# Early loads of an FFT mixing kernel in another order, spread over sixteen DMA engines, in smaller reads, with the interleaving retimed

## The chip, the core and the metric

The kernel runs on one core of a Trainium2 chip. The time is the device time of one execution in microseconds (us), lower is better. One core has five engines that matter here: TensorE (PE in the profile; its weight loads are PEld), VectorE (DVE), ScalarE (ACT), GpSimd (POOL) and SyncE (SP). All share 16 DMA engines. A DMA is issued by SyncE, ScalarE or GpSimd, whose issues show as SPq, ACTq and POOL lines. In the DMA view, queue q0 carries what GpSimd issues, q1 what SyncE and q10 what ScalarE issues.

## The reference

For 8 images of 3136 tokens with 256 channels, a real Fourier transform over the tokens is multiplied by a filter and transformed back. Then comes a token mixer of rank 32, and a two-layer channel mixer with a residual:

```python
def _attn_ref(x, filt_r, filt_i):
    X = np.fft.rfft(x, axis=1)
    Y = X * (filt_r + 1j * filt_i)[None, :, :]
    return np.fft.irfft(Y, n=x.shape[1], axis=1).astype(np.float32)

def _moe_ref(x, U, V, w_ch1, w_ch2):                # x is the result of the above
    xt = x.transpose(0, 2, 1)
    h = xt @ U @ V                                  # rank 32 over the tokens
    u = x + h.transpose(0, 2, 1)
    ch = np.maximum(u @ w_ch1, 0.0) @ w_ch2         # 256 -> 1024 -> 256
    return (u + ch).astype(np.float32)
```

## The kernel before

3136 is 64 x 49, and both transforms are done as two stages of matmuls. The images go through in five units, counted from 0: image 1 alone is unit 0, image 2 alone is unit 1, then come three pairs. Each unit passes through these parts:

- **stage 1** (`f1`): load `x`, one matmul stage, store the result to a scratch tensor in DRAM (`ct1`; the trace writes `ct<-asb`, `ct<-al`).
- **mid stage** (`mid`): load it back as `a2` (in the trace `a<-ct`), multiply by the matrix `tf2`, multiply on VectorE by the filters `fab` (giving `uv`), multiply by the matrix `g3`, evacuate on ScalarE to `esb`, store to a second scratch tensor (`ct<-esb`). There are 32 such steps per unit.
- **low rank** (`low_rank`): load all of that unit back (`eh<-ct`), 24 matmuls into one small result, and two more copies, `hp` and `h1`.
- **groups**: the last inverse stage (`pu`, evacuated to `ut`), first channel matmul with ReLU (`phh`, `h`), second channel matmul (`pc`), store of the output. A unit has 7 groups if it is one image and 13 if it is two: g00 to g06 are image 1, g07 to g13 image 2, g14 to g26, g27 to g39 and g40 to g52 the pairs.

The groups are the steady work. Each full group has 8 steps, and a plan deals the next units' stage 1, mid stage and low rank onto these steps. For image 1 nothing can hide them: until its low rank is done there is no group to run.

These are the parts that the change and the argument touch. `hold(dst, src)` copies one element on VectorE, so that a load into `dst` can't be issued before `src` is there.

```python
def load_x(u, c, after=None):                       # x in 8 KB reads per row
    ...
        t = sb.tile([128, 8 * DM], F16, tag="x", bufs=4, name="x")
        if after is not None:
            hold(t[0:1, 0:1], after)
        nc.gpsimd.dma_start(t, dram(x.tensor, (u.b[0] * SEQ + 8 * c) * DM,
                                    [[NR * DM, 64], [st, 2], [1, 8 * DM]]))
def load_filters(a, z):                             # one of four parts of the filters, in pieces of 25 and 24 rows
    ...
def mirror_filters(a, z):                           # both halves once more, swapped: 1.6 MB inside SBUF
    nc.sync.dma_start(fab[0:NR, 1, a:z, :], fab[NR:98, 0, a:z, :])      # NR = 49
    nc.sync.dma_start(fab[NR:98, 1, a:z, :], fab[0:NR, 0, a:z, :])
load_filters(PARTS[0], PARTS[1])                    # part 0 at the very start, behind x
...
def second_loads(src):                              # at image 1's first a2
    for i in range(2, 4):
        load_part(i, src)                           # filter parts 2 and 3
    ...                                             # three small ones, then the rest of tf2 and g3
def third_loads(src):                               # at image 1's 11th multiply
    ...                                             # usb, vnat, w1sb, w2sb
# [f1: tf2 and g3 of the first 8 steps between the stage-1 stores; filter part 1 at stage 1's last evacuation]

# [low_rank, loads of image 1 in two parts]
if u.n == 0:
    a = 32
    for c in range(3):
        load(c, 0, a)
    load_l(0, a)
    yield
for c in range(3):
    load(c, a)
load_l(a)

# [main program, image 1]
for i in range(33):
    next(mids[0])
    if i == 24:
        next(ranks[0])                              # first part of the low-rank loads
...
next(ranks[0])                                      # second part
fourth_loads(units[0].held[64:65, 0, 0:1])          # x of image 2
...
hold(fab[0:1, 1, 0, 0:1], units[0].h1[64:65, 0:1])
hold(fab[64:65, 1, 0, 0:1], units[0].h1[64:65, 0:1])
mirror_filters(0, NK)                               # after image 1's h1

# [plan: generator, number of pieces, first step, last step; S = first step of each unit = 0, 49, 98, 196, 294]
deal(f1s[1], 7, 4, 11)
deal(mids[1], 33, 17, 33)
deal_f1(units[2], 12, (0, 2, 6, 7))
deal(mids[2], 33, 44, S[2] - 29)
deal_rank(units[1], 34, S[1] - 7)
deal_rank(units[2], S[2] - 28, S[2] - 7)
for u in units[3:]:
    deal_f1(u, S[u.n - 1] - (38 if u.n == 3 else 60), (1, 7))
    deal(mids[u.n], 33, S[u.n - 1] + (21 if u.n == 3 else 3), S[u.n] - 36)
    deal_rank(u, S[u.n] - 35, S[u.n] - 8)
```

## Time and profile before

| | |
|---|---|
| median of 3 runs | 629.87 us (628.38 to 631.92) |
| TensorE busy | 552.8 us, 88% of the span |
| TensorE's wait for image 1's low-rank loads | 10.3 us, ends at 65.4 |
| TensorE's wait behind image 2's x | 3.9 us, ends at 84.4 |
| TensorE's wait for the third low-rank loads | 10.5 us, ends at 248.6 |

The page of the kernel before cuts the span into 40 slices of 15.7 us. Each digit is a busy share in tenths. PEclk is the granted TensorE clock in tenths.

```profile
...
PE   3294576999699993989999999999999999999997
...
PEclk9558576999979997989999999999999999999999
DMA  9898979999835749868567787455433862331112
...
```

From the nineteenth slice on TensorE is full. The idle time lies before that, and there the DMA engines are full instead. The granted clock is 0.5 to 0.7 in seven of the slices up to the sixteenth, most of them slices in which TensorE idles or the next ones.

The view of waits gives, for one engine and a window, what the waiting line was released by: total us, number of times, longest. This is TensorE in the kernel before, from 60 to 180 us:

```profile
...
PE ph L476 <- DMA eh<-ct_0: 11.6, 3, 10.3
PE ph L476 <- DMA eh<-ct_1: 4.1, 3, 2.6
PE pf L304 <- DVE ut L539: 3.9, 1, 3.9
...
```

And the same view from 225 to 275 us:

```profile
...
PE ph L476 <- DMA eh<-ct_2: 10.5, 1, 10.5
...
```

Nearly all of it is the low rank waiting for its loads (`eh<-ct`). The third line is the start of stage 1 of a later unit behind a VectorE copy. What that copy waited for is seen in the chain and in VectorE's timeline below.

The chain of work that ended last, in order of time: start, length, what.

```profile
...
16.96 6.25 DMA ct_0<-al
23.25 4.47 DMA a_161<-ct_0
...
69.42 13.53 DMA x<-in_x_dram
...
```

The last store of stage 1 lands at 23.2 and the first load back starts. At 69.42 begins a load of x for image 2 that lands 13.5 us later.

In the view of the timeline a bracket gives the idle time before an instruction and what ended it.

```profile
...
83.05 0.14 DVE L174 COPY x<-x 1x1 f16<-1x1 f16 x1 [9.28 <-DMA x<-in_x_dram]
83.12 1.20 DVE L539 CAST ut<-pu 128x1024 f16<-128x1024 f32 x1
...
```

The one-element copy `x<-x` is the hold that lets the next unit's x load go only after image 2's third x tile. It waits 9.3 us for that tile, and the evacuation `ut` of the next group, ready by then, comes behind it in VectorE's program order.

### The profile page before, as it was taken

To read this page: it belongs to the slowest core of one execution; us is meant where nothing else is said; L and a number is where in the kernel's file an instruction comes from. 1 tells how busy PE (TensorE), PEld (TensorE's weight loads), DVE (VectorE), ACT (ScalarE), POOL (GpSimd) and SP (SyncE) were. 2 spreads that over 40 slices of the span, in tenths; PEclk is the share of its full clock that TensorE was granted. 3 is DMA by queue.
4 is the path that set the end of the run, shared out by engine and by line. 5 is a ranking of instruction groups with operands and counts; after the bars stand their busy time and mean duration, and the time that the engine had idled before them with its cause. 6 is when DMAs were issued, how large, how long until landed. Compare 5 with 4: busy or idle time off the path is not lost.

```text
span 629.3 us, 10769 instructions
## 1 busy us (share of the span) xinstructions
PE 552.8 (88%) x4350; PEld 388.0 (62%) x4350; DVE 330.0 (52%) x390; ACT 334.6 (53%) x623; POOL 41.7 (7%) x62
## 2 busy tenths in 40 slices
PE   3294576999699993989999999999999999999997
PEld 0183242767456661657766676777677767777776
DVE  5274222786278870263888743576866325333332
ACT  0043232667156662546667665665766655666663
POOL 3345110100000000000000000000000000000000
PEclk9558576999979997989999999999999999999999
DMA  9898979999835749868567787455433862331112
GB/s 176 230 205 193 214 183 236 246 250 244 244 119 161 216 81 286 208 166 227 171 187 173 208 245 249 156 148 187 120 131 119 239 202 83 99 100 67 66 67 102
DMA packets 68002, 110.18 MB, mean 175 GB/s; under 512 B 5549, under 2 KB 49438, under 8 KB 66604
## 3 DMA queue, kind: packets, MB, share of 16 engines
q1 hardware_dynamic: 36240, 81.17, 41.2%
q0 software_dynamic: 7312, 15.91, 15.8%
q10 hardware_dynamic: 24400, 12.41, 6.9%
q8 instruction: 34, 0.56, 0.4%
q14 instruction: 16, 0.13, 0.1%
HBM read 72.38 MB, written 51.38 MB: 197 GB/s over the span
## 4 chain that ended last, share of the span: by engine, by line
PE 73%; DMA 16%; issue 4%; DVE 3%; ACT 2%; ACTq 1%; POOL 0%; SPq 0%; POOLq 0%; DVEq 0%
PE phh L550 25%; PE pc L590 24%; PE pe L360 8%; PE pz L382 5%; PE pu L532 3%; PE pc L564 3%; DMA x<-in_x_dram 3%; PE pf L304 3%; DMA ct_3<-asb 2%; DMA g_78<-g 2%; DMA eh<-ct_1 2%; ACTq L320 1%; DMA eh<-ct_2 1%; DMA ct_0<-asb 1%; PE ph L476 1%
## 5 line engine op out<-in xcount | busy, mean ns | idle before, releaser
L550 PE MATMUL phh<-ut,w1sb 128*128 128x512 f16 (+2 forms) x848 | 251.7, 377 | 3.5 <-DVE ut L539 3.0
L397 DVE TENSOR_TENSOR uv<-pz,fab 98x1024 f16<-98x1024 f32 (+1 forms) x128 | 137.8, 1087 | 35.3 <-PE pz L382 34.8
L600 DVE COPY och<-pc 128x512 f32<-128x512 f32 x96 | 66.3, 690 | 165.8 <-PE pc L564 162.6
L550 PEld LDWEIGHTS <-w1sb 128*128 128x128 f16 x848 | 105.6, 146 | 36.7 <-issue 16.7
L366 ACT CAST esb<-pe 98x512 f16<-98x512 f32 (+1 forms) x160 | 79.5, 501 | 64.6 <-PE pe L360 57.0
L360 PE MATMUL pe<-uv,g_78 98*98 98x512 f16 (+1 forms) x320 | 85.7, 353 | 1.4 <-DMA g_78<-g 0.8
L539 DVE CAST ut<-pu 128x1024 f16<-128x1024 f32 (+1 forms) x51 | 59.9, 1174 | 21.6 <-PE pu L532 21.4
L564 PE MATMUL pc<-idn,ut 128*128 128x128 f16 x394 | 54.8, 220 | 0.0
L360 PEld LDWEIGHTS <-g_78 98*98 98x98 f16 x320 | 41.3, 132 | 19.4 <-issue 5.6
L564 PEld LDWEIGHTS <-ut 128*128 128x128 f16 x394 | 38.7, 98 | 6.7 <-issue 0.3
L382 PEld LDWEIGHTS <-tf_74 98*98 98x98 f16 x160 | 21.7, 136 | 20.2 <-DMA a_163<-ct_0 15.3
L304 PE MATMUL pf<-x,wf_64 128*128 128x512 f16 x84 | 27.9, 402 | 6.8 <-DVE ut L539 6.3
L476 PE MATMUL ph<-eh,ut_94 128*32 128x512 f16 (+1 forms) x120 | 10.7, 384 | 26.2 <-DMA eh<-ct_0 11.6
L167 POOL DMA_DIRECT2D x<-in_x_dram x24 | 14.1, 602 | 266.5 <-PE pf L304 225.1
L309 DVE CAST asb<-pf 128x1024 f16<-128x1024 f32 x21 | 25.6, 1219 | 11.5 <-PE pf L304 8.9
L307 ACT CAST asb<-pf 128x1024 f16<-128x1024 f32 x21 | 21.3, 1013 | 10.7 <-PE pf L304 6.7
L390 DVE TENSOR_TENSOR uv<-pz,fab 98x512 f16<-98x512 f32 x32 | 20.9, 687 | 5.1 <-PE pz L387 2.9
L476 PEld LDWEIGHTS <-ut_94 128*32 128x32 f16 x120 | 3.3, 97 | 31.6 <-issue 20.7
L366 ACT ACT_TABLE_LOAD x1 | 1.3, 1283 | 30.2 <-DVE uv L390 30.2
L382 PE MATMUL pz<-a_161,tf_74 98*98 98x256 f16 x8 | 3.2, 403 | 15.2 <-DMA a_163<-ct_0 14.9
L532 PEld LDWEIGHTS <-eb_97 96*128 96x128 f16 x256 | 10.3, 100 | 7.5 <-issue 4.7
L486 ACT CAST hp<-ph 128x512 f16<-128x512 f32 (+1 forms) x5 | 2.5, 501 | 23.1 <-PE ph L483 23.1
(1427 smaller groups left out, 1046.2 us busy)
## 6 DMA issues: line engine op xcount, KB each, us to landing
out_dram<-och SPq DMA_DIRECT2D x48, 512.0 KB
x<-in_x_dram POOLq DMA_DIRECT2D x24, 512.0 KB, 8.0
ct_2<-esb SPq DMA_DIRECT2D x16, 196.0 KB
ct_3<-esb SPq DMA_DIRECT2D x16, 196.0 KB
ct_4<-esb SPq DMA_DIRECT2D x16, 196.0 KB
ct_2<-asb ACTq DMA_DIRECT2D x6, 512.0 KB
ct_3<-asb ACTq DMA_DIRECT2D x6, 512.0 KB
eh<-ct_2 SPq DMA_DIRECT2D x6, 512.0 KB
```

Source lines behind the costliest of these rows:

```text
L304: nc.tensor.matmul(pf[:, i, :], wx, u.x[c][:, r:r + 2, :], start=True, stop=True)
L309: nc.vector.tensor_copy(dst, pf)
L360: nc.tensor.matmul(pe[0:98, 0:bd], g3[:, (2 * k + l) * 98:(2 * k + l + 1) * 98], uv[:, l * bd:(l + 1) * bd], start=(l == 0), stop=(l == 1))
L366: nc.scalar.copy(st["esb"][:, i, :], pe[0:98, 0:bd])
L382: nc.tensor.matmul(pz[0:98, 0:bd], wz, a2[c][:, i, :], start=True, stop=True)
L397: nc.vector.tensor_mul(uv.rearrange("p (f b d) -> p f b d", f=2, b=nb), zin, fin)
L532: nc.tensor.matmul(pu[:, dh, 64 * i:64 * i + 64], e2[0:96, d0:d0 + 128], sv[0:96, 64 * r:64 * r + 64], start=(i == 0), stop=True, skip_gro ...
L539: nc.vector.tensor_copy(gr.ut[:, :, 0:n].rearrange("p h (c q s) -> p h c q s", q=64, s=2), pu[:, :, 0:n].rearrange("p h (c s q) -> p h c q ...
L550: nc.tensor.matmul(ph[:, 0:n], w1v[:, dh, :, t], gr.ut[:, dh, 0:n], start=(dh == 0), stop=(dh == 1))
L564: nc.tensor.matmul(o[:, dh * 128:dh * 128 + 128], gr.ut[:, dh, t0:t0 + n], idn, start=False, stop=(dh == 1), skip_group_check=True)
L590: nc.tensor.matmul(o, gr.h[tt][:, i * 128:(i + 1) * 128], w2sb[:, tt * DM:(tt + 1) * DM], start=(tt == 0), stop=False, skip_group_check=True)
L600: nc.vector.tensor_copy(dst, gr.pc.rearrange("p (j d) -> p j d", j=2))
```

## The change

The intent is to take loads out of the crowded early stretches in which TensorE waits, to make each spread over more DMA engines, and to move pieces of the plan apart that seemed to collide:

- Start: filter part 0 and the first tf2 and g3 pieces come behind stage 1's last evacuation; filter part 1 at the first a2, parts 2 and 3 at the second and seventh multiply, the rest of tf2 and g3 at the first multiply. Filters load 24 rows and then one row. Half of the first unit's evacuations go to ScalarE.
- w1 and w2 are loaded late, behind the low-rank loads. Those come in three parts of 32, 16 and 16 rows.
- The mirror copies 48 rows and then one. x comes in 4 KB reads, two per tile. Two copies of h1 go to GpSimd.
- The plan is retimed, most of all for units 2 and 3.

```diff
 # load_x
+                hold(t[0:1, 4 * DM:4 * DM + 1], after)
+            for i in range(2):
+                nc.gpsimd.dma_start(t[:, 4 * i * DM:4 * (i + 1) * DM], ...   # [1, 4 * DM] per row
 # load_filters
-                fab[p0:p0 + 25, 0, a:a + n, :],
+                fab[p0:p0 + 24, 0, a:a + n, :],          # the 25th rows in load_filter_rows()
-    def mirror_filters(a, z):
-        nc.sync.dma_start(fab[0:NR, 1, a:z, :], fab[NR:98, 0, a:z, :])
-        nc.sync.dma_start(fab[NR:98, 1, a:z, :], fab[0:NR, 0, a:z, :])
+    def mirror_filters():
+        for a, z in ((0, 48), (48, NR)):
+            nc.sync.dma_start(fab[a:z, 1, :, :], fab[NR + a:NR + z, 0, :, :])
+            nc.sync.dma_start(fab[NR + a:NR + z, 1, :, :], fab[a:z, 0, :, :])
-    load_filters(PARTS[0], PARTS[1])
 # f1, unit 0
-                        nc.vector.tensor_copy(dst[:, i, :], pf)
+                        (nc.scalar.copy if i else nc.vector.tensor_copy)(dst[:, i, :], pf)
+        if u.n == 0:
+            first_loads(al[0:1, 0:1])                    # tf2 and g3 of the first 8 steps
+            load_part(0, asb[0:98, 4, 0:1])
 # mid, unit 0
-            second_loads(a2[0][0:1, 0, 0:1])
+            second_loads(a2[0][:, 0, 0:1])               # filter part 1 and three small ones
+            if u.n == 0 and k == 0:
+                second_matrices(uv[:, 0:1])              # the rest of tf2 and g3
+            if u.n == 0 and k in (1, 6):
+                load_part(2 if k == 1 else 3, uv[:, 0:1])
 # low_rank, unit 0
-            a = 32
-            for c in range(3):
-                load(c, 0, a)
-            load_l(0, a)
-            yield
+            for z in (32, 48):
+                for c in range(3):
+                    load(c, a, z)
+                load_l(a, z)
+                a = z
+                if z == 48:
+                    load_w1(eh[0][64:65, 0, 0:1])
+                yield
 # main program and plan                      (S = 0, 49, 98, 196, 294)
-        if i == 24:
+        if i in (22, 29):
             next(ranks[0])
-    deal(f1s[1], 7, 4, 11)
-    deal(mids[1], 33, 17, 33)
-    deal_f1(units[2], 12, (0, 2, 6, 7))
-    deal(mids[2], 33, 44, S[2] - 29)
+    deal(f1s[1], 7, 5, 12)
+    deal(mids[1], 33, 18, 34)
+    deal_f1(units[2], 17, (0, 2, 6, 7))
+    deal(mids[2], 33, 50, S[2] - 27)
-    deal_rank(units[2], S[2] - 28, S[2] - 7)
+    deal_rank(units[2], S[2] - 26, S[2] - 6)
     for u in units[3:]:
-        deal_f1(u, S[u.n - 1] - (38 if u.n == 3 else 60), (1, 7))
-        deal(mids[u.n], 33, S[u.n - 1] + (21 if u.n == 3 else 3), S[u.n] - 36)
-        deal_rank(u, S[u.n] - 35, S[u.n] - 8)
+        if u.n == 3:
+            deal_f1(u, S[2] - 38, (1, 7), (S[2] - 32, S[2] - 16))      # leaves out 16 steps
+        else:
+            deal_f1(u, S[u.n - 1] - 60, (1, 7))
+        deal(mids[u.n], 33, S[u.n - 1] + (40 if u.n == 3 else 3), S[u.n] - (30 if u.n == 3 else 36))
+        deal_rank(u, S[u.n] - (29 if u.n == 3 else 35), S[u.n] - 7)
 # [cut: ranks of unit 1 one step later; w2 and x held on other parts of eh; copies of h1 on GpSimd]
```

## The prediction

> **What bounds the kernel.** Median 629.87 us. The table of stages shows TensorE 99 to 100% busy from 300 us to 600 us (94% in 250 to 300): nothing to win there. The first 250 us hold nearly all of its idle time. The waits and the chain name it: 6.6 us for the first x; 15 us (12.6 to 27.9) for stage 1's stores and the a2 load; 10.3 us (55.1 to 65.4) for the low-rank load of the first image; 3.9 us at 80.5 behind the second image's x; about 6 us in 99 to 105, where ScalarE's queue is stuck issuing stores; about 6 us in 155 to 175 (second low-rank load, chain 9.9 us); 10.5 us before 248.6 (third low-rank load). After such gaps the granted clock is half: it is 0.61 in 27 to 50, 0.63 in 70 to 83 and 0.66 in 95 to 110.
>
> In these gaps the DMA engines are 80 to 100% busy, so order and spread of transfers matter, not compute.
>
> **What the change does.**
> 1. Start. In 9 to 24 us the filter loads hold 50% of the engines while the first stores, issued at 9.7, trickle until 14; the last store lands at 23.25. Part-0 and part-1 filters (0.8 MB in SBUF), tf2 and g3 parts (0.5 MB) now follow. Half the evacuations move from VectorE (0.68 us each, back to back) to ScalarE. Estimate: a2 loads 4 us earlier, stage 2 starts near 24.
> 2. First image's mid stage: filter parts stay just in time; g3 may again stall a microsecond or two (0.8 before). w1 and w2, which took most of the engines at 46 to 55 (software queue 52% in 46 to 62), leave that stretch. The last low-rank part shrinks from 32 to 16 rows. Estimate: low rank starts near 57 instead of 65.4, 8 us in all including step 1's 4.
> 3. The filter mirror: the trace's packets run on about 7 engines in 82 to 90. 49 rows give k = 7 and 48 give 16 (the Trainium skill, "DMA: Bandwidth & Descriptors", section on why a DMA increments its semaphore by 16), and this trace agrees. The x loads for image two (13.5 us in the chain) no longer share seven clogged engines. With the later stage 1 of unit 2 this recovers perhaps 6 of the 10 us lost in 80 to 110.
> 4. Retimed plan: a2 of unit 2 leaves the second low-rank stretch (4 us); unit 3's stage 1 skips the third one (8 us).
> 5. Costs: doubled x issues (0.58 us each, GpSimd, off the path); two 32x2048 copies on GpSimd instead of 0.68 us on VectorE, off the path; unit 2's mid stage is squeezed from 25 steps to 21 and unit 3's from 40 to 28, where 33 multiplies of 1.23 us bring VectorE to TensorE's level or above: 5 us lost. w2 and x now come late in a row: 3 us of new waits.
>
> Sum: 8 + 6 + 4 + 8 - 5 - 3 = 18, plus some 3 us from a clock that recovers earlier.
>
> **Prediction: 609 us, range 595 to 621 (8 in 10). Faster by over 2%: 0.77; within 2%: 0.20; slower: 0.03.**
>
> **What would show it.** First stage-2 matmul at about 24 us; first low-rank matmul about 57; mirror on the DMA view under 8 us; no wait over 3 us for the third low-rank load; more waits on VectorE's uv in the mid stages of units 2 and 3; TensorE busy time a little lower through the clock.
>
> **What would make it wrong.** New waits for filter parts or w1/w2; 2 KB x packets losing rate; the third low-rank load still late; gains given back because VectorE limits the squeezed mid stages.

## More of the kernel before

The order of instructions in the traces isn't exactly that of the plan; where it matters, it is read from the trace.

In the DMA view between 26 and 50 us, the columns after the count are KB and median us to landing:

```profile
...
fab<-in_filt_r_dram POOLq DMA_DIRECT2D x1, 100.0 KB, 7.7
...
fab<-in_filt_i_dram POOLq DMA_DIRECT2D x1, 84.0 KB, 13.1
...
```

Pieces of 84 to 100 KB take 8 to 13 us among the other loads of that stretch.

## The result, and the profile after

The changed kernel's median is 665.52 us (662.89 to 668.12, four runs), beside 629.36 for the kernel before. The ratio is 1.057 (95% interval 1.052 to 1.062): slower by 5.7%, where 3.3% faster had been predicted. The profiled executions were a little slow for their kernels (631.07 and 668.12 us), so the traces' spans differ by 37.0 us (629.3 to 666.3) where the medians differ by 36.2.

The slices of the page after are 16.7 us long:

```profile
...
PE   3257237699859999739999999899999999999997
...
PEclk9968577799969999868999999899999999999999
DMA  8896997869967545975788836853562563233112
...
```

TensorE's early idle time has grown, at slices 5 and 6, and the gap that was at slice 16 is now at 17 and 18, deeper in sum. TensorE's busy time rose by 10.8 us (552.8 to 563.6) for the same 4350 matmuls, and the other 26.2 of the 37.0 us are idle time. Where the longer busy time comes from wasn't followed up; the PEclk row shows lower clocks in slices 17 to 19, where the row of the kernel before has them in 16 and 18.

The waits of TensorE in the kernel after, from 60 to 180 us:

```profile
...
PE ph L499 <- DMA eh<-ct: 13.0, 1, 13.0
PE pf L328 <- DVE ut L562: 12.8, 1, 12.8
PE pz L398 <- DMA a<-ct: 4.1, 1, 4.1
...
```

And from 240 to 300 us, which holds the third low rank:

```profile
...
PE ph L499 <- DMA eh<-ct: 11.2, 5, 3.6
...
```

Not one of the waits that the change was meant for has gone. The first low-rank wait is 13.0 instead of 10.3 us, the wait behind image 2's x is 12.8 instead of 3.9, and the third low-rank wait is 11.2 in five pieces instead of 10.5 in one.

The chain of the kernel after, in order of time:

```profile
...
15.48 9.09 DMA ct<-asb
24.70 4.43 DMA a<-ct
...
59.19 5.51 DMA ct<-esb
67.32 2.66 DMA ct<-esb
70.59 5.63 DMA eh<-ct
79.70 21.19 DMA x<-in_x_dram
...
```

The next table gives milestones, read from the traces: starts of instructions, but ends for the two last multiplies; a group starts with its first ReLU. It is the map for all that follows. The first column is the kernel before, and the others are differences to it. The kernels e1 and so on are those of the experiments below; e14 and e13 each add to e5 alone. Every column is one execution. How far two executions of one program lie apart is seen in e15, whose instructions stand in the same order as those of the kernel before: -0.6 at g01, +2.4 at g07, +1.0 at g14 and +1.7 at g27. Differences of 2 to 3 us say little.

| us | before | after | e1: old plan | e5: + late mirror | e14: + early filters | e13: + two parts | e12: + both | e8: plan alone |
|---|---|---|---|---|---|---|---|---|
| image 1, first multiply | 28.5 | +1.5 | +2.7 | +1.8 | +1.0 | +2.1 | +0.6 | +0.2 |
| image 1, last multiply | 54.4 | +7.8 | +9.2 | +8.2 | +0.4 | +8.3 | +0.5 | +0.1 |
| first low-rank matmul | 65.4 | +10.2 | +10.8 | +11.4 | +6.0 | +5.7 | -0.6 | -0.2 |
| group g01 | 86.3 | +18.0 | +18.2 | +6.8 | +1.5 | +6.4 | -0.4 | -0.3 |
| group g07 | 176.7 | +23.8 | +23.0 | +9.4 | +8.9 | +8.2 | +2.4 | +4.0 |
| unit 2, last multiply | 229.1 | +30.9 | +21.9 | +8.7 | +8.0 | +8.1 | +1.6 | +11.1 |
| group g14 | 273.5 | +28.6 | +20.0 | +7.4 | +6.4 | +5.9 | +0.2 | +7.1 |
| group g27 | 403.5 | +37.1 | +18.7 | +7.0 | +6.1 | +6.1 | -0.7 | +14.4 |

Down the column of the kernel after there are three places where the loss grows: the mid stage of image 1 (about 8 us by its end, 10 with the low rank), the stretch to g01 (8 more), and from there on the units that the new plan moved (19 more). From g27 on nothing changes.

**The mid stage of image 1.** VectorE's timeline of the kernel after:

```profile
...
29.16 0.68 DVE L177 COPY fab<-a 1x1 f16<-1x1 f16 x4 [13.22 <-DMA a<-ct]
...
31.38 0.67 DVE L177 COPY fab<-uv 1x1 f16<-1x1 f16 x4
...
36.62 0.67 DVE L177 COPY fab<-uv 1x1 f16<-1x1 f16 x4
43.43 2.06 DVE L406 TENSOR_TENSOR uv<-pz,fab 98x512 f16<-98x512 f32 x3 [6.14 <-issue]
...
```

At 37.3 VectorE is done with the first eight multiplies and the holds for filter part 3. The ninth multiply needs part 1 of the filters, which could be issued only after the hold at 29.16. It comes 6.1 us late. The same is seen on GpSimd, whose bracket names the load:

```profile
...
31.32 0.66 POOL L199 DMA_DIRECT2D fab<-in_filt_i_dram  x1
...
43.95 0.70 POOL L199 DMA_DIRECT2D fab<-in_filt_i_dram  x1 [5.15 <-DMA fab<-in_filt_i_dram]
...
```

Part 1's four pieces are issued from 29.59 to 31.98, and part 2 and most of part 3 right behind. The issue at 43.95 waited 5.2 us for a filter piece to land. By the DMA view of this stretch the pieces took 8 to 12 us (medians), much as in the kernel before. Part 1's own four took 3.0, 3.2, 6.2 and 12.0 us: the last one, issued at 31.32, landed at 43.35, and the multiply began at 43.43. In the kernel before part 1 had been issued from 15 us on, and the wait did not exist.

**The low rank of image 1.** SyncE's timeline, its issues alone, in the kernel before:

```profile
...
53.85 2.24 SPq L368 DMA_DIRECT2D ct_0<-esb  x3
61.62 1.80 SPq L448 DMA_DIRECT2D eh<-ct_0  x3
...
```

And in the kernel after:

```profile
...
59.19 0.98 SPq L384 DMA_DIRECT2D ct<-esb  x2
...
64.75 1.84 SPq L468 DMA_DIRECT2D eh<-ct  x3
...
67.32 0.34 SPq L384 DMA_DIRECT2D ct<-esb  x1
...
69.99 1.81 SPq L468 DMA_DIRECT2D eh<-ct  x3
...
```

Before, SyncE issues the last stores of the mid stage in a row, and the second half of the low-rank loads waits for them alone. After, the second part (64.75) waits for a store of 59.19 to land, and the last store (67.32), which has nothing to do with it, is issued only behind it, by SyncE's program order. The third part waits for that store in turn (69.99). The chain shows just these pieces: store 59.19, store 67.32, load 70.59. From the last multiply to the first low-rank matmul the kernel before takes 11.0 us and the kernel after 13.5.

**Image 2's x.** VectorE's timeline after:

```profile
...
100.98 0.20 DVE L177 COPY x<-x 1x1 f16<-1x1 f16 x2 [19.04 <-DMA x<-in_x_dram]
101.11 1.20 DVE L562 CAST ut<-pu 128x1024 f16<-128x1024 f32 x1
...
```

The hold waits 19.0 us for x, and behind it `ut` is late, which is TensorE's 12.8 us. The x tile was issued at 79.7 instead of 69.4, since the low rank was late, and then took 21.2 instead of 13.5 us. The DMA view of the stretch 88 to 94 gives each queue's packets, MB and share of the 16 engines:

```profile
...
q1 hardware_dynamic: 67, 0.80, 90.5%
q0 software_dynamic: 65, 0.12, 16.4%
...
```

q0 is x, q1 almost only the mirror. The mirror holds 90% of the engines, and x gets 0.12 MB in 6 us, in about as many packets (65 and 67).

**The plan.** In unit 2 the plan deals the mid stage onto fewer steps (21 instead of 25); in the trace it starts at 205.9 instead of 171.1 and ends at 259.9 instead of 229.1. From its end to g14 both kernels need much the same time (44.4 us before, 42.2 after), so the later end is passed on. In unit 3 the same happens again. The view of stretches gives start and end, the length, then the busy us (and instructions) of PE, PEld, DVE, ACT and POOL, the granted clock, the DMA share and GB/s. For 55 us of unit 2's mid stage, before:

```profile
...
175.00:230.00 55.00, 53.90 (x344) 33.30 (x344) 46.62 (x44) 34.27 (x66) 1.00 (x2) 0.94 0.51 150
...
```

And after:

```profile
...
205.00:260.00 55.00, 54.28 (x359) 33.75 (x359) 46.53 (x44) 34.47 (x66) 1.19 (x2) 1.00 0.49 144
...
```

VectorE is no busier after the change than before it (46.5 and 46.6 of 55 us), and TensorE is full in both.

### The profile page after: what moved, and what is told of

Same layout as the page of the kernel before. It is cut to its first block, busy times and chain, and to the rows that moved or that the text cites. A ratio compares the mean times of both kernels' runs of the same rounds, so it can differ in the third digit from the quotient of the medians.

```text
span 666.3 us, 10847 instructions
## 1 busy us (share of the span) xinstructions
PE 563.6 (85%) x4350; PEld 390.0 (59%) x4350; DVE 327.6 (49%) x401; ACT 338.2 (51%) x630; POOL 61.2 (9%) x90
## 4 chain that ended last, share of the span: by engine, by line
PE 67%; DMA 21%; DVE 5%; ACT 3%; issue 2%; POOL 1%; SPq 1%; ACTq 0%; DVEq 0%; POOLq 0%
PE phh L573 23%; PE pc L613 20%; PE pe L376 8%; DMA eh<-ct 7%; PE pz L398 5%; DMA x<-in_x_dram 4%; DMA ct<-al 3%; PE pf L328 3%; PE pc L587 3%; PE pu L555 3%; DMA ct<-esb 2%; DMA a<-ct 2%; DVE eb L441 2%; DMA ct<-asb 1%; DVE ut L562 1%
## 5 line engine op out<-in xcount | busy, mean ns | idle before, releaser
L576 ACT ACTIVATE h<-phh 128x512 f16<-128x512 f32 (+2 forms) x424 | 237.1, 566 | 169.7 <-PE phh L573 164.4
L613 PE MATMUL pc<-w2sb,h 128*128 128x256 f16 x1536 | 242.1, 276 | 1.0 <-ACT h L576 1.0
L613 PEld LDWEIGHTS <-h 128*128 128x128 f16 x1536 | 146.6, 99 | 74.1 <-issue 7.4
L376 PE MATMUL pe<-uv,g 98*98 98x512 f16 (+1 forms) x320 | 84.8, 351 | 0.6 <-ACT esb L382 0.4
L398 PE MATMUL pz<-a,tf 98*98 98x512 f16 (+1 forms) x160 | 56.4, 355 | 27.6 <-DMA a<-ct 18.4
L376 PEld LDWEIGHTS <-g 98*98 98x98 f16 x320 | 41.1, 133 | 18.7 <-issue 4.7
L555 PEld LDWEIGHTS <-eb 96*128 96x128 f16 x768 | 32.5, 100 | 17.7 <-DVE eb L441 6.4
L328 PE MATMUL pf<-x,wf 128*128 128x512 f16 x84 | 27.8, 403 | 14.5 <-DVE ut L562 14.1
L555 PE MATMUL pu<-sv,eb 96*128 96x64 f16 x768 | 35.7, 197 | 5.0 <-DVE eb L441 3.7
L499 PE MATMUL ph<-eh,ut 128*32 128x512 f16 (+1 forms) x120 | 11.2, 408 | 32.9 <-DMA eh<-ct 32.7
L398 PEld LDWEIGHTS <-tf 98*98 98x98 f16 x160 | 21.5, 135 | 22.7 <-issue 16.2
L331 ACT CAST asb<-pf 128x1024 f16<-128x1024 f32 x21 | 21.3, 1013 | 15.5 <-PE pf L328 15.3
```

What stands on the lines that cost most here:

```text
L328: nc.tensor.matmul(pf[:, i, :], wx, u.x[c][:, r:r + 2, :], start=True, stop=True)
L376: nc.tensor.matmul(pe[0:98, 0:bd], g3[:, (2 * k + l) * 98:(2 * k + l + 1) * 98], uv[:, l * bd:(l + 1) * bd], start=(l == 0), stop=(l == 1))
L398: nc.tensor.matmul(pz[0:98, 0:bd], wz, a2[c][:, i, :], start=True, stop=True)
L555: nc.tensor.matmul(pu[:, dh, 64 * i:64 * i + 64], e2[0:96, d0:d0 + 128], sv[0:96, 64 * r:64 * r + 64], start=(i == 0), stop=True, skip_gro ...
L576: nc.scalar.activation(h[:, 0:n], ph[:, 0:n], RELU)
L613: nc.tensor.matmul(o, gr.h[tt][:, i * 128:(i + 1) * 128], w2sb[:, tt * DM:(tt + 1) * DM], start=(tt == 0), stop=False, skip_group_check=True)
```

## The experiments

I took the reading above as theory A: the loss has three sources, the loads of image 1, the mirror beside x, and the plan, and the plan costs time on its own. The rival B for each source was that it does not cost by itself but only passes on a lateness made elsewhere. For the plan in particular B says that the new plan still helps, and that only a late start hides it. The letters in the texts stand for the theory under test and its rival in that run.

In the short diffs, a minus line is of the kernel after (or before, where said), and the plus line what the experiment has in its place. The times are medians; each ratio is against the kernel before in the same rounds, with its 95% interval.

### e1: the old plan under the new loads

```diff
-    deal(f1s[1], 7, 5, 12)        # and all other lines of the new plan
+    deal(f1s[1], 7, 4, 11)        # the plan of the kernel before, unchanged
```

> The changed kernel with only the retimed plan (the steps at which later units' stages are dealt out) put back to that of before; everything of the early loads stays changed. Theory A (the retimed plan itself costs: the mid stage of unit 2 starts 10.9 us later than the groups around it, the low-rank stage of units 2 and 3 then ends late): some 13 us back, about 652 us. Theory B (the plan fits the new loads and saves, the loss is all in the first 110 us): time rises by up to 10 us, to 668 to 676 us.

Measured: 646.86 us, 1.027 (1.019 to 1.035). The new plan costs about 18.7 us of the 36. In the table the +18.2 of g01 is +23.0 at g07 and +18.7 at g27: under the old plan a late start is in the end neither recovered nor made worse. The filter wait is there too, and here the bracket on VectorE names it (line numbers are of this kernel):

```profile
...
44.91 2.06 DVE L442 TENSOR_TENSOR uv<-pz,fab 98x512 f16<-98x512 f32 x3 [6.43 <-DMA fab<-in_filt_i_dram]
...
```

### e2: the mirror with 49 rows again

```diff
-        for a, z in ((0, 48), (48, NR)):
+        for a, z in ((0, NR),):
```

> The changed kernel with the filter mirror back in two transfers of 49 rows. Theory A (spread over 16 engines with 16 KB packets, the mirror starves the second image's x loads, which landed at 101 us, 21 us after the issue): x lands near 92 us, about 657 us in all. Theory B (x is late because its 2 KB packets lose against any larger ones, or because w2 stands in front of it): unchanged within 2 us, 664 to 668 us.

Measured: 660.80 us, 1.048 (1.039 to 1.056), and g01 at +17.4 instead of +18.0. I had suspected that the mirror crowds x out because it now runs on all engines. That falls: on seven engines x is as late, with the third tile at 100.4. A gain of some 5 us appears only later in the program; I can't explain it, and end to end it is not clear of the noise (1.048 against 1.057, 1.0% on either side).

### e3: the low-rank loads in two parts

```diff
-            for z in (32, 48):
+            for z in (32,):            # w1 then held on the first part
```

> The changed kernel with the first image's low-rank loads in two parts as before (w1 held on the first part). Theory A (the loads of the second of three parts stand on SyncE's in-order queue ahead of the last store of the mid stage, which is ready at 62.9 us and issued at 67.3): first low-rank matmul 3 to 5 us earlier than 75.6 us, about 661 us in all. Theory B (the last part is shorter with three parts, so the split saves): 666 to 670 us.

Measured: 661.00 us, 1.049 (1.043 to 1.054). The run doesn't tell what it should. To keep w1 late I held it on the first part, and that hold sat on VectorE in the middle of the mid stage, so image 1's last multiply came at +12.6 instead of +7.8. What two parts gained was lost there. e13 does this properly.

### e4: the filters in the old order

```diff
+    load_filters(PARTS[0], PARTS[1])   # at the start, and parts 1 to 3 where they were before
-            load_part(0, asb[0:98, 4, 0:1])
```

> The changed kernel with the filters, tf2 and g3 loaded when and in the row counts they were before (25 and 24 rows), all else changed. Theory A (putting filters and matrices late moved no store forward and made the mid stage wait: 4.2 us on VectorE's multiply, 2.4 us on tf2): first multiply near 28.5 us, no wait over 1 us in the first mid stage, about 659 us in all. Theory B (the stores gain as intended and the late start comes from elsewhere): 666 us or more.

Measured: 655.11 us, 1.039 (1.033 to 1.046). Image 1's last multiply is at +1.2 instead of +7.8, and g01 at +11.6 instead of +18.0. The late loads are shown to be the cause of the loss in the mid stage. This edit, and those of e13 and e14, puts back tf2, g3, the row counts and the number of holds together with the time of the filters; "late filters" below stands for all of it. The bracket in e1 names a filter piece. The first multiply came at 29.7, beside 30.1 with late filters and 28.5 before: there was no gain to lose at the start.

### e5: old plan, and the mirror after x

The mirror is held on the third x tile of image 2, and issued later in the program order.

```diff
-    hold(fab[0:1, 1, 0, 0:1], units[0].h1[64:65, 0:1])
-    hold(fab[64:65, 1, 0, 0:1], units[0].h1[64:65, 0:1])
-    mirror_filters()
 # in the step loop, after unit 2's first load_x
+    hold(fab[0:1, 1, 0, 0:1], units[1].x[2][0:1, 0, 0:1])
+    hold(fab[64:65, 1, 0, 0:1], units[1].x[2][64:65, 0, 0:1])
+    mirror_filters()
```

> The run with the old plan (646.9 us) with one thing more: the filter mirror waits for the second image's third x tile to land, as its result is first read some 30 us later. Theory A (x and mirror share the engines packet by packet, and the mirror's 16 KB packets leave little to x's 2 KB ones: x drops to 20 GB/s beside it): x lands near 90 us instead of 101, about 638 us in all. Theory B (x is late by w2 and its own order alone): no change, 645 to 649 us.

Measured: 639.41 us, 1.018 (1.013 to 1.022). The x tile lands at 90.2, g01 is at +6.8 instead of +18.2, and end to end 0.9% of the time is won against e1 (1.018 against 1.027). In the DMA view of 82 to 92 us the queues have changed places:

```profile
...
q0 software_dynamic: 980, 1.69, 91.8%
q1 hardware_dynamic: 95, 0.51, 16.9%
...
```

Now x has 92% of the engines and moves 1.69 MB in 10 us. The mirror beside x is the cause of the loss between 80 and 101 us.

### e6: x in 8 KB reads again, with the old plan

```diff
-            for i in range(2):         # two reads of 4 KB
+            for i in range(1):         # one of 8 KB
```

> The run with the old plan (646.9 us) with x back in single reads of 8 KB (4 KB packets in SBUF). Theory A (packet size sets x's share beside the mirror): x lands 3 to 6 us earlier than 101 us, about 642 us in all; the start is unchanged or up to 1 us earlier. Theory B (packet size is harmless): 645 to 649 us.

Measured: 649.73 us, 1.032 (1.027 to 1.036), against e1's 1.027: no gain. Yet the packets tell why x yields to the mirror. This is a sum over the trace's packet records in the two halves of 88 to 96 us, with the mirror running in all three kernels:

```
                     x: packet size, rate              queue with the mirror: packet size, rate
e1 (4 KB reads)      1.8 KB, 18 to 25 GB/s             12 to 13 KB, 140 to 153 GB/s
e6 (8 KB reads)      3.7 to 3.9 KB, 37 to 58 GB/s      11 to 12 KB, 129 to 176 GB/s
e2 (4 KB, 49 rows)   1.3 to 1.7 KB, 18 to 41 GB/s      8 to 13 KB, 136 to 145 GB/s
```

The Trainium skill, "DMA: Bandwidth & Descriptors", section "Queues, rings and completion order", says that each DMA engine goes round the queues for which it has work, one packet each. By that, x would get 1.8 of every 1.8 + 12.5 KB, an estimate of 13%, with the small reads, and 3.7 of 3.7 + 12.5 KB, 23%, with the large ones. The runs show 11 to 14% and 22 to 25%. So the 4 KB reads did halve x's share beside the mirror. But x landed only 2.1 us earlier with the large reads (99.0 against 101.1), and it had also been issued 2.1 us earlier (77.7 against 79.8). From issue to the landing that the hold waits for, both took 21.4 us, though in e6 that is the whole tile and in e1 its first half. The 2.1 us were lost again by the start of unit 3 (its first a2 load: +19.1 against e1's +18.6). The larger share is shown, a gain of time is not.

### e7: all loads of image 1 in the old order, old plan

```diff
 # e1, and the filters as in e4, and the low rank in two parts as in e3
```

> The run with the old plan (646.9 us) with filters, matrices and low-rank loads back in their old order and parts; late w1 and w2, x in 4 KB reads, the 48-row mirror and the moved copies stay. If the first mid stage's waits and the three parts cost the 8.8 us seen at the first ReLU: about 637 us, first ReLU near 74 us or earlier, since w1 and w2 no longer fill the engines. If late w1/w2, x reads or the mirror cost it: 643 us or more.

Measured: 640.75 us, 1.018 (1.012 to 1.025). The hold of w1 on the first part costs here as in e3: the trace shows VectorE stopped from 49.6 to 54.5, and TensorE with it from 50.2 to 55.3. g00 came at +3.7 and g01 at +12.7. The direction is clear, the size is not. e12 repeats it without this fault.

### e8: the new plan alone on the kernel before

```diff
 # kernel before
-    deal(f1s[1], 7, 4, 11)        # and all other lines of the old plan
+    deal(f1s[1], 7, 5, 12)        # the plan of the kernel after
```

> The kernel before with the retimed plan alone. Theory A (the plan's loss of 18.6 us is its own, independent of the loads): about 648 us. Theory B (the plan only fails on top of late early loads): 630 us or less.

Measured: 645.92 us, 1.027 (1.024 to 1.030). This settles the matter of the plan: with none of the other changes, and image 1 as early as before, the plan alone costs 2.7%. The wait that it was to avoid is back as five waits:

```profile
...
PE ph L537 <- DMA eh<-ct: 11.0, 5, 3.4
...
```

From the table: unit 2's last multiply is 11.1 us late, g14 7.1 us, g27 14.4 us. TensorE's idle time, summed from the instruction records between milestones, shows the exchange: from g07 to g13 it falls from 11.4 us in the kernel before to 0.8, but from g13 to g14 it rises from 2.3 to 15.3, and from g20 to g27 from 0.0 to 3.7.

### e9: the late mirror alone on the kernel before

```diff
 # kernel before, with the change of e5
```

> The kernel before (629 us) with one thing changed: the filter mirror, still 49 rows, waits for the second image's third x tile. Theory A (mirror and x collide in the kernel before too, there for the 3.9 us that TensorE waits behind x at 80.5): x lands near 80 us instead of 83, 3 to 4 us in all, about 626 us. Theory B (the collision only hurts where x comes late): 628 to 631 us; if the mirror then comes too late for the next mid stage, more.

Measured: 633.83 us, 1.003 (0.9995 to 1.007): nothing gained. g01 came 4.3 us earlier, as it should, since x landed at 79.1 instead of 83.0. But the mirror then ran while ScalarE was issuing the stores of stage 1. Two lines of ScalarE's timeline:

```profile
...
88.36 15.62 ACTq L366 DMA_DIRECT2D ct<-asb  x2
104.03 1.01 ACT L353 CAST asb<-pf 128x1024 f16<-128x1024 f32 x1 [15.19 <-issue]
...
```

ScalarE spent 15.6 us on issuing two stores, and its next evacuation waited behind them. TensorE's waits show it:

```profile
...
PE pf L376 <- ACT asb L353: 13.2, 1, 13.2
...
```

That moving the large transfer out of one collision moved it into another is my reading. The mirror's packets ran from 81.0 to 99.9, through most of this time. But in the kernel before, too, ScalarE's issues of two such pairs, from 93.7 on and with the mirror over since 91.1, took 4.1 and 5.2 us beside x of the next unit. How much of the 15.6 us is the mirror's is not shown.

### e10 and e11: the new plan of unit 2 alone, and of unit 3 alone, on the kernel before

```diff
 # e10, kernel before
-    deal_f1(units[2], 12, (0, 2, 6, 7))
-    deal(mids[2], 33, 44, S[2] - 29)
-    deal_rank(units[2], S[2] - 28, S[2] - 7)
+    deal_f1(units[2], 17, (0, 2, 6, 7))
+    deal(mids[2], 33, 50, S[2] - 27)
+    deal_rank(units[2], S[2] - 26, S[2] - 6)
 # e11, kernel before: the lines of the new plan for u.n == 3
```

> The kernel before with only unit 2's part of the retimed plan (stage 1 five steps later, mid stage from step 50 to 71 instead of 44 to 69, low-rank stage 2 steps later). Theory A (the low-rank chain follows the end of the mid stage, so a mid stage that ends later ends the unit later, whatever waits it avoids before): 3 to 5 us slower, about 633 us. Theory B (the loss in the plan-only run is from the one-step shifts of unit 1): within 1.5 us of before.

> The kernel before with only unit 3's part of the retimed plan (stage 1 skips 16 steps, which pushes the mid stage from steps 119 to 159 to steps 138 to 166, low-rank stage 6 steps later). Theory A: the 10.5 us wait before unit 2's low-rank matmuls shrinks, but unit 3's low-rank stage ends late and gives back more, about 7 us slower in sum, 636 us. Theory B (removing the wait is worth its length): 620 us.

Measured: e10 637.83 us, 1.009 (1.004 to 1.013); e11 637.96 us, or 637.53 without its slow execution, 1.006 (1.001 to 1.012). Both halves cost. In e11 my idea worked at first: with unit 3's stage 1 out of the way, g13 starts 8.6 us earlier and g20 9.7 us earlier than in the kernel before. The gain is given back in unit 3, whose mid stage now ends 11.6 us later, and g27 is 7.3 us late. Together they are 1.5%, beside 2.7% for the whole plan, a difference of 1.2% with 0.8% on either side. In the traces nothing is missing: at g27 they are +6.7 and +7.3, together 14.0, beside e8's +14.4. Neither edit has the one-step moves of unit 1 and of the end of units 3's and 4's low rank, but in e10's trace unit 1's mid stage already stands in e8's order. So the two halves account for all, or nearly all, of the plan's loss; what the other moves add is not resolved.

### e12: old loads, old plan, late mirror, with the rest of the change left in

```diff
 # kernel after with the old plan, the filters in the old order, the low rank in two parts, the late mirror,
 # and w1 held on the last low-rank part:
+        if u.n == 0:
+            load_w1(eh[0][64:65, 0, 0:1])      # after the second part is issued
```

> What is left of the change once the plan, the filter order and the three low-rank parts are back as before and the mirror waits for x: late w1 and w2 (w1 held on the last low-rank part, not in the middle of the mid stage as in the two earlier runs with two parts, where that hold stalled VectorE for 5 us), x in 4 KB reads, 48 rows, the evacuations and copies moved to other engines. If plan, filter order, three parts and mirror collision are all the causes: first ReLU at 74 us as before and 625 to 630 us. If late w1 and w2 or the rest cost by themselves: 633 us or more.

Measured: 631.30 us, 0.999 (0.994 to 1.003). What is left in it (x in 4 KB reads, evacuations on ScalarE, w1 and w2 late, the mirror of 48 rows, copies on GpSimd) neither costs nor gains as a whole. The first low-rank matmul comes at 64.7, beside 65.4 in the kernel before, so taking w1 and w2 out of the stretch before it gained nothing that the traces resolve. The sum can hide opposite parts, and the traces show some. In e9 and e12 the mirror comes after x, and x is asked for from 68.4 and 68.2 us. In e9 the third tile was there at 79.1 and g01 came 4.3 us early; in e12, where x stands behind w2 and comes in 4 KB reads, the tile was there at 82.2 and g01 came 0.4 us early. And TensorE waited 1.8 us for w1. I ran none of these parts alone.

### e13 and e14: one of the two returned at a time

```diff
 # e13: e12 with the filters late, as in the kernel after
 # e14: e12 with the low rank in three parts, as in the kernel after
```

> The late-mirror run (old plan, 639.4 us) with the first image's low-rank loads in two parts and w1 held on the last part, so that no hold stands in the mid stage; the new filter order stays. Theory A (three parts cost some 3.4 us, as SyncE's queue keeps the last store behind a load that waits): about 636 us, gap from the mid stage's end to the first low-rank matmul 11 us instead of 14. Theory B (the filter order alone makes the 8 us between 639.4 and 631.3): 639 us.

> The late-mirror run (old plan, 639.4 us) with the old filter and matrix loads, three low-rank parts kept. Theory A (filters cost 5 us, parts 3.4): about 634.5 us. Theory B (filters alone): 631 us, as the run with both undone (631.3).

Measured: e13 637.28 us, 1.011 (1.008 to 1.014); e14 634.36 us, 1.006 (1.002 to 1.009). Beside e12, the late filters add 7.8 us at the end of image 1's mid stage (+8.3 against +0.5 in the table). The three parts add 6.6 us at the first low-rank matmul without delaying the mid stage at all. With both, in e5, that matmul is at +11.4. Of the 6.6 us of e14 only 1.9 are left at g01, and at g27 they are 6.8; how they grow again in between I didn't resolve. The profiled execution of e14 was the slowest of its six, 2.5 us above their median. As with the filters, the edit of the three parts brings small things with it (where `u_hat` and the holds of w1 and w2 stand).

The ratios of e1, e5, e13, e14 and e12 give the bill. The interval of a step, worked out from those of its two ratios, is 0.9% on either side for the first two steps and 0.6% for the others. The runs also come from several chips, each beside its own kernel before.

| step | ratio before | ratio after | part of the time |
|---|---|---|---|
| new plan undone (after to e1) | 1.057 | 1.027 | 3.0%, 19 us |
| mirror moved behind x (e1 to e5) | 1.027 | 1.018 | 0.9%, 6 us |
| filters in the old order (e5 to e14) | 1.018 | 1.006 | 1.2%, 8 us |
| low rank in two parts (e14 to e12) | 1.006 | 0.999 | 0.7%, 4 us |

The us are the percentages of 629 us. In this order the steps lead back to the time of the kernel before. End to end the mirror's step is only just clear of the noise; what shows it is x's landing and g01 in the traces of e1 and e5. Taken the other way round, from e5 to e13 to e12, the parts are worth 0.7% and the filters 1.2%: within the noise the two add up.

### e15 and e16: the opposite of the new plan

If an earlier end of unit 2's mid stage is what the third low-rank wait needs, it must start earlier rather than later.

```diff
 # kernel before; e15, and in brackets e16
-    deal(mids[2], 33, 44, S[2] - 29)
-    deal_rank(units[2], S[2] - 28, S[2] - 7)
+    deal(mids[2], 33, 44, S[2] - 32)           # (42, S[2] - 33)
+    deal_rank(units[2], S[2] - 31, S[2] - 7)   # (S[2] - 32)
```

> The kernel before with unit 2's mid stage dealt out over steps 44 to 66 instead of 44 to 69, and its low-rank stage 3 steps earlier: the opposite of the retimed plan. Theory A (the chain from the end of this mid stage to the first ReLU of unit 2, some 44 us in both kernels, decides): 3 to 4 us faster than before. Theory B (VectorE limits, the squeezed stage gains nothing): within 1 us of before.

> As the last, with steps 42 to 65 and the low-rank stage 4 steps earlier. Theory A: 4 to 6 us faster than before, unless its loads then meet unit 1's low-rank loads. Theory B: within 1 us.

Measured: e15 631.32 us, 1.002 (0.998 to 1.006), no gain. But e15 tested nothing: in its trace all instructions of every engine stand in the same order as in the kernel before (only semaphore waits that start together change places), so the edit of the plan didn't reach the program that ran. It is a repeat of the kernel before, and neither theory is touched. e16 625.71 us, 0.993 (0.988 to 0.997), faster than both kernels. Here the order did change: counted in pairs of first channel matmuls, unit 2's low rank runs over pairs 95 to 107 instead of 98 to 110. Its mid stage starts 4.8 us earlier, the first low-rank matmul of unit 2 comes 9.7 us earlier and g14 5.5 us. The low-rank wait is shorter:

```profile
...
PE ph L539 <- DMA eh<-ct: 7.3, 3, 3.5
...
```

So 7.3 us in three pieces instead of 10.5 in one. It is a gain of 0.7%, found by moving in the opposite direction.

## Why the prediction was wrong

The prediction was 609 us, with 0.03 for slower. It was wrong in its sign. What it said of the state before was right: the idle time is early, loads cause it, and TensorE is full from 300 us on. It failed in two ways. A load sent later, into a stretch that is just as full, needs the same 8 to 13 us to land, and its user then waits (steps 2 and 3). And work moved out of a wait ends later, and with it the unit (step 4, the largest part). Step by step:

1. **"a2 loads 4 us earlier, stage 2 starts near 24."** Failed. The first a2 load was at 24.70 instead of 23.25, and the first multiply 1.5 us later. The chain shows where: the last store to land was issued 1.5 us earlier (15.48 against 16.96), and took 9.1 instead of 6.3 us. Filters, tf2 and g3 were held on stage 1's evacuations, not on the stores' landing, so they were issued together with the last stores, from 14.65 us on. They were moved beside the stores, not behind them. That this alone delayed the start is not shown: with the loads back in their old places (e4) the first multiply still came at 29.7 instead of 28.5.
2. **"filter parts stay just in time"; "low rank starts near 57".** This is the first step that failed by its mechanism. The parts were late by 6.1 us, and the first low-rank matmul came at 75.6. The trace of before had the number: 8 to 13 us per piece. Part 1, issued up to 32 us, could not be there at 37.3. e13 and e14 put the late filters at 1.2%. The idea that the third part of 16 rows would shorten the wait failed as well: two rounds of store, then load, in one issue queue, cost 0.7% (e14). And the removal of w1 and w2, to which I gave a part of the gain, came with a first low-rank matmul only 0.7 us earlier in e12, while x then stood behind w2.
3. **"no longer share seven clogged engines ... recovers perhaps 6 of the 10 us".** The first half was right: 48 rows did run on 14 to 15 engines and 49 on 6 to 9 (from the queue's busy share, 88 to 96 us, e1 and e2), as the skill says. (The Trainium skill, "DMA: Bandwidth & Descriptors", section "Why a DMA increments its semaphore by 16 and not by 1": the largest number up to 16 that divides the row count, so 7 and 16.) But "mirror on the DMA view under 8 us" didn't come true. From the first to the last of its packets it took 13.3 us on all engines, 13.4 us on seven in e2 and 12.3 us in the kernel before: one packet of 16,384 bytes took 1.32 us instead of 0.62 (medians of the packet records). Nor was x earlier with seven engines (e2). So the number of engines wasn't what held x up; the mirror beside it was (e5). The wait grew from 3.9 to 12.8 us; undone by e5, this is 0.9%. Why the mirror hit x harder than before is only argued: image 2's third tile was issued 1.7 us before the mirror (79.7 and 81.4), where it had been 4.2 us before it (69.4 and 73.6), w2 now stands ahead of x, and the smaller reads halved x's share, so more of x met the mirror's large packets.
4. **"a2 of unit 2 leaves the second low-rank stretch (4 us); unit 3's stage 1 skips the third one (8 us)."** The largest miss: predicted 12 us of gain, measured 3.0%, 19 us, of loss (e1), 2.7% by itself (e8). The second low-rank wait was 6.5 us instead of 4.1. e11 shows that the 8 us for the third were really gained at g13, and that they were lost again in unit 3. A piece of work moved out of a wait must be done later, and there it delays the end of its own mid stage, on which the next low rank waits.
5. **"bring VectorE to TensorE's level or above: 5 us lost".** This did not happen. TensorE waited nowhere for `uv` in the mid stages of units 2 and 3, was busy for 53 of unit 2's 54 us and 54 of unit 3's 55 us, and both stages took less time than before (54.0 instead of 58.0 us, 54.7 instead of 63.1). In the trace unit 2's stage isn't even squeezed: it runs over 34 pairs of first channel matmuls, and over 33 before. The cost is not in the stage; it is that it starts 35 us later and ends 31 us later. The other cost that the prediction named, 3 us for w2 and x late in a row, is about what e9 and e12 differ by (the third tile at 79.1 and 82.2), with the smaller reads mixed in.
6. **What would make it wrong:** "New waits for filter parts", "the third low-rank load still late" and "2 KB x packets losing rate" were named, and happened, the last without a loss of time that e6 could show. "VectorE limits the squeezed mid stages" did not. To be slower in the end was given three chances in a hundred. I named the risks without working out a single one, though the landing times for the first lay in the trace.

What stays open: the gain of some 5 us in e2, which appears only after image 2; the 2 to 7 us that the stretch from g01 to g07 adds in several kernels (in e14 +1.5 becomes +8.9), of which some 3 us may be the one execution of the kernel before, since its repeat e15 shows them too; what w2 ahead of x and the 4 KB reads each cost; the 10.8 us of longer busy time; and what the smallest moves of the plan add.

## What to carry to other kernels

Before a load is moved later, take the time that its like needs from issue to landing in the same crowded stretch, and subtract it from the moment of use; a hold on the producer's copy doesn't order the load behind the producer's store. Before work is dealt to other steps, follow to which later stage its end is passed on, and count a wait as gone only when that stage is no later. See in the trace that the order of instructions has changed at all before reading a result (e15). Keep a large copy inside SBUF away from a load that somebody waits for: here x, in packets of 1.8 KB, got 11 to 14% of the bytes beside it. Then see whom it meets instead.

## What the Trainium skill lacked or had wrong

- "DMA: Bandwidth & Descriptors", section "Queues, rings and completion order": arbitration packet by packet agrees with the runs, but the page doesn't say what follows, that packet size sets the share. x got 11 to 14% of the bytes with packets of 1.8 KB and 22 to 25% with 3.7 to 3.9 KB, beside a copy whose queue had packets of 11 to 13 KB on average.
- The same page, table in section "SWDGE vs HWDGE vs iDMA": a packet is preferably at most 4096 bytes. The table stands under the path of DMAs issued by GpSimd; the page gives no size for the packets of a copy issued by SyncE, and the mirror inside SBUF ran in 96 packets of 16,384 bytes.
- The same page, section "Why a DMA increments its semaphore by 16 and not by 1": the number of engines agreed (14 to 15 busy with 48 rows, 6 to 9 with 49). But the rule "Use all 16 engines" of the section "Rules for kernel authors" brought nothing for this copy inside SBUF: 13.3 us on 16 engines, 13.4 us on 7 (e2), with x beside both. One packet of 16,384 bytes took 1.32 us and 0.62 us.
- The same page, section "Anatomy of one DMA — SWDGE (gpsimd) path": the fit of 2.0 us plus the bytes over 436 GB/s would give, as an estimate, 2.2 us for a filter piece of 100 KB. Under load the pieces took 8 to 13 us. The fit has no term for the load of the queues.
- No page gives a time for an issue on a loaded chip; the DMA page, section "Issuing engines are not separate DMA queues", calls it usually small beside the DMA itself. ScalarE spent 15.6 us on issuing two stores, for most of it with the mirror running (e9), where the next two took 2.7 us.
